# 21 additions and subtractions move from VectorE to GpSimd, and every queue gets a new order

## The chip, the cores and the metric

The kernel runs on one core of a Trainium2 chip. The core has a matrix engine (TensorE, PE in the profile, its weight loads PEld), three engines for elementwise work (VectorE = DVE, ScalarE = ACT, GpSimd = POOL) and a queue that issues DMAs (SyncE = SP). Each engine works through its own queue in order; a semaphore makes one wait for another. The metric is the device time of one execution in microseconds. Before the change it is 566.58 us, the median of three runs (565.62 to 568.13).

## The reference

Banded attention with block summaries, followed by an MLP with GELU, all in float32:

```python
q, k, v: (4, 8, 768, 64)                      # batch, heads, positions, dims
k_sum = k.reshape(B, H, 24, 32, 64).max(axis=3);  v_sum = v.reshape(B, H, 24, 32, 64).mean(axis=3)
scores_l = q @ k.T / 8, only where |i - j| < 16        # the band
scores_s = q @ k_sum.T / 8 + log(32)                   # 24 summaries for each position
a = softmax over both together
x = (a @ concat(v, v_sum)) as (3072, 512)
g = gelu(x @ w_in)                            # w_in (512, 2048)
out = g @ w_out                               # w_out (2048, 512)
```

## The kernel before

Each float32 factor of a large matmul is split into a high and a low half of 16 bits, and a product takes three matmuls (high × high, high × low, low × high). The high parts are casts, on ScalarE or GpSimd; the low parts are a difference (`*_lo`), on VectorE. So every product hangs on a chain: a read of PSUM, a cast, a difference, then TensorE.

The attention is cut into 24 units (four heads, 256 positions): `load_q`, `load_k`, `load_v` fetch, `q_hi`, `q_lo`, `k_hi`, `k_lo` split, `scores` multiplies, `maximum`, `exponent`, `recip` make the softmax, `p_hi` or `split_hi` and `p_lo` or `split_lo` split it, `turn` transposes it by DMA into `pt`, `values` multiplies with v. Two units make a chunk of 256 rows of x, two chunks a pair. For pairs 2 to 5 the first MLP product is done by Strassen's scheme: seven products (`product p j m`) instead of eight, of sums of the four blocks of x (`sx_add`) and of w_in (`t_add`); `keep` and `h_add` put the results together. Before that, `phase1` does a chunk's block with 24 matmuls and `phase1h` half of one; the first units use float32 matmuls. GELU gives g, `g_hi` and `g_lo` split it, and `phase2 c i` sums a quarter of an output block (12 matmuls of 512 columns). For the last pair the second product is done by the same scheme: sums of g (`s_add j n`, with `s_hi` and `s_lo` for the split) and of w_out (`u_add`), products `s_product m j` and `s_last`. `warm` are dummy matmuls at the start.

The four sums of a set are made in place, one out of the other: S1 into block 22, S3 into block 21, S2 from S1 into block 11, S4 from S2 into block 12. So the four `s_add j n` (n = 1, 3, 2, 4), and likewise the four `sx_add`, are a chain.

Nothing schedules this: the text `ORDER` lists 1,585 steps, and the program issues each step's instructions in that order, so that each engine's queue is the list restricted to that engine. SyncE's DMAs stand in the same list. The steps that the change touches are `q_lo` (line 723), `sx_add` (893) and `s_add` (1039); all three end in one VectorE instruction of 128 partitions × 512 columns.

Of the kernel before, what the change touches and what calls it, by code (L numbers as in the profile page):

```python
# [78 lines left out]
p_turn 0 0, wi_hi 7 1, maximum_p 1, wh_bits 6 1 1, wh_bits 6 1 2, wi_lo 1 1, wh_bits 6 0 1, exponent_p 1, wi_hi 1 0,
wh_bits 6 0 2, wi_lo 7 1, wh_bits 7 0 2, recip 1, p_norm 1, p_turn 0 1, warm 4 5, sum_vt 0, mean_vt 0, load_v 0,  # L80
load_v 1, fetch_w_in 3, fetch_w_in 5, load_q 3, sum_vt 1, wi_lo 1 0, wi_bits 2 0, load_neg, wi_hi 7 0, wi_bits 2 1,
wi_lo 7 0, f_mask 2, scores 2, p_keep 0 1, wi_hi 6 0, maximum_p 2, wi_lo 6 0, p_keep 0 0, s_load_vs 0, mean_vt 1,
warm 5 1, values 0, load_vs 1, take_hi 0, wi_hi 6 1, take_lo 0, wi_bits 3 0, wi_bits 2 2, wi_bits 3 1, wi_bits 3 2,
p_turn 1 0, p_turn 1 1, p_keep 1 0, phase1h 0 6 0, p_keep 1 1, exponent_p 2, wi_hi 2 0, wi_bits 5 0, recip 2,
values 1, phase1h 0 1 0, phase1h 0 7 0, take_hi 1, wi_hi 2 1, s_norm 2, wi_hi 3 0, wi_lo 2 0, take_lo 1, wi_bits 5 1,
f_mask 3, scores 3, fetch_w_in 4, wi_bits 5 2, t_add 3 0, maximum_p 3, wi_lo 2 1, wi_bits 4 0, wi_lo 3 0, wi_lo 6 1,
load_v 2, p_turn 2 0, phase1h 0 1 1, p_turn 2 1, wi_hi 5 1, p_keep 2 0, wi_hi 5 0, p_keep 2 1, exponent_p 3, load_q 4,
fetch_w_in 0, load_vs 2, phase1h 0 2 0, values 2, phase1h 0 7 1, phase1h 0 6 1, wi_hi 3 1, take_hi 2, gelu 0 1,
wi_bits 0 0, wi_bits 4 1, recip 3, p_norm 3, wi_bits 4 2, wi_hi 4 1, wi_bits 0 1, wi_bits 0 2, phase1h 0 3 0,
gelu 0 7, f_mask 4, scores 4, fetch_w_out 4, load_v 4, load_v 3, fetch_kx 3 0, load_q 5, fetch_w_out 0, wi_hi 4 0,  # L90
load_vs 3, s_load_vs 4, take_lo 2, maximum_p 4, wi_lo 4 0, wi_lo 3 1, p_turn 3 0, g_hi 0 7, p_keep 3 0, p_turn 3 1,
p_keep 3 1, phase1h 0 2 1, values 3, v_hi 4, gelu 0 2, wi_hi 0 0, take_hi 3, g_lo 0 7, wi_lo 4 1, phase1h 0 4 0,
take_lo 3, phase1 1 3, phase1 1 1, exponent_p 4, wo_bits 4 0, wi_hi 0 1, wi_lo 5 0, wo_bits 4 1, wi_lo 0 0,
wo_bits 4 2, wo_hi 4, wi_lo 5 1, recip 4, t_add 0 0, v_lo 4, wi_lo 0 1, f_mask 5, scores 5, wo_lo 4, gelu 1 1,
g_hi 0 2, wo_bits 0 0, g_lo 0 2, phase1h 0 4 1, wo_bits 0 1, wo_bits 0 2, g_hi 0 1, gelu 1 3, gelu 0 6, gelu 0 4,
g_hi 1 1, g_hi 1 3, g_hi 0 6, phase1 1 0, phase1 1 6, wo_hi 0, phase1h 0 0 0, phase1h 0 5 0, phase1h 0 3 1,
phase1h 0 5 1, phase1h 0 0 1, g_hi 0 4, split_hi 4, g_lo 1 1, g_lo 0 6, wo_lo 0, fetch_w_out 1, wo_bits 1 0,
wo_bits 1 1, wo_bits 1 2, g_lo 0 1, g_lo 1 3, load_v 5, load_q 7, s_load_vs 5, fetch_w_out 7, fetch_w_out 5, wo_hi 1,
# [5 lines left out]
g_lo 0 4, g_lo 0 5, wo_lo 3, fetch_w_out 6, wo_bits 6 0, wo_bits 6 1, g_lo 1 2, wo_bits 6 2, g_hi 1 5, wo_hi 6,
maximum_p 5, exponent_p 5, fetch_k 1 0, wo_lo 6, load_k 7, load_k 6, fetch_k 1 1, g_lo 1 5, split_lo 4, v_lo 5,
turn 4 1, prep_k 1 0, s_k_hi 7, recip 5, phase2 1 1, phase2 0 0, phase2 1 0, phase2 0 1, s_q_hi 6, k_hi 6, s_q_hi 7,
phase2 0 2, phase2 0 4, phase2 0 3, phase2 0 6, phase2 0 5, phase2 1 3, q_lo 7, prep_k_end 1 0, k_lo 6, q_lo 6,
k_sums 1 0, store 0 0, split_hi 5, scores 6, values 4, prep_k 1 1, add_mask 6, k_lo 7, split_lo 5, take_hi 4,
take_lo 4, prep_k_end 1 1, maximum 6, k_sums 1 1, exponent 6, phase2 1 5, phase2 1 2, phase2 0 7, scores 7,
fetch_v 1 0, load_v 6, load_k 8, fetch_v 1 1, turn 5 0, turn 5 1, load_q 8, load_k 9, load_q 9, prep_v 1 0,  # L110
prep_v 1 1, values 5, take_hi 5, load_vs 6, fetch_v 3 0, s_q_hi 8, s_k_hi 8, add_mask 7, take_lo 5, q_hi 9, s_k_hi 9,
recip 6, k_lo 8, prep_kx 3 0, k_lo 9, maximum 7, q_lo 8, split_hi 6, v_hi 6, store 0 1, phase2 1 4, phase1 2 2,
phase1 2 6, phase1 2 4, scores 8, gelu 2 2, v_lo 6, split_lo 6, g_lo 1 7, turn 6 0, put 0 0, load_v 7, turn 6 1,
load_vs 7, load_q 10, fetch_v 2 0, prep_v 3 0, add_mask 8, exponent 7, g_hi 2 2, phase1 2 3, gelu 2 3, phase2 1 7,
store 1 1, gelu 2 6, g_lo 2 2, recip 7, v_hi 7, maximum 8, p_norm 7, q_lo 9, p_hi 7, values 6, phase1 2 0, phase1 2 1,
scores 9, load_k 10, load_k 11, put 0 1, turn 7 0, v_lo 7, load_v 8, load_q 11, prep_v 2 0, p_lo 7, add_mask 9,
k_hi 10, k_hi 11, turn 7 1, q_hi 11, s_q_hi 10, k_lo 10, phase1 2 5, phase2 1 6, gelu 2 4, take_hi 6, take_lo 6,
values 7, exponent 8, g_hi 2 4, g_hi 2 6, g_lo 2 4, g_lo 2 6, gelu 2 1, g_hi 2 1, store 1 0, load_vs 8, phase1 2 7,
maximum 9, recip 8, q_lo 10, scores 10, v_hi 8, gelu 2 0, take_hi 7, gelu 2 5, split_hi 8, v_lo 8, take_lo 7,
split_lo 8, phase1 3 7, phase1 3 5, phase1 3 0, phase1 3 2, exponent 9, fetch_k 2 0, g_lo 2 1, k_lo 11, prep_k 2 0,  # L120
g_hi 2 5, g_hi 2 0, load_v 9, load_q 12, q_lo 11, t_add 2 0, t_add 0 1, g_lo 2 5, add_mask 10, g_lo 2 0, load_vs 9,
v_hi 9, gelu 3 0, gelu 2 7, g_hi 2 7, gelu 3 5, g_hi 3 0, recip 9, maximum 10, v_lo 9, put 1 0, load_k 12,
fetch_k 2 1, prep_k 2 1, g_lo 3 0, prep_k_end 2 1, turn 8 0, p_norm 9, fetch_v 2 1, turn 8 1, load_v 10, fetch_v 3 1,
exponent 10, prep_k_end 2 0, g_hi 2 3, k_sums 2 0, phase2 2 1, phase1 3 3, scores 11, values 8, gelu 3 3, g_hi 3 3,
x_take 8, phase1 3 1, load_q 13, prep_v 2 1, recip 10, p_norm 10, g_lo 2 3, phase2 2 3, phase2 2 5, sx_hi 2 0,
q_hi 12, p_hi 9, p_lo 9, q_lo 12, k_hi 12, t_add 2 1, g_lo 2 7, load_k 13, turn 9 0, s_p_hi 10, load_vs 10, turn 9 1,
gelu 3 2, gelu 3 7, add_mask 11, gelu 3 1, v_hi 10, maximum 11, s_k_hi 13, s_q_hi 13, k_lo 12, v_lo 10, p_lo 10,
phase2 2 7, sx_lo 2 0, k_sums 2 1, g_hi 3 5, store 2 1, t_add 0 2, t_add 0 3, t_add 2 2, t_add 3 1, values 9,
load_k 14, load_v 11, scores 12, phase1 3 4, g_lo 3 5, prep_v 3 1, add_mask 12, exponent 11, s_k_hi 14, k_lo 13,
q_lo 13, recip 11, load_vs 11, turn 10 0, v_hi 11, x_take 9, k_lo 14, phase2 2 0, sx_hi 2 1, split_hi 11, maximum 12,  # L130
product 2 0 1, phase2 2 2, phase1 3 6, keep 2 0 0, sx_lo 2 1, turn 10 1, load_q 14, q_hi 14, q_lo 14, split_lo 11,
load_q 15, put 1 1, product 2 0 2, values 10, turn 11 0, turn 11 1, scores 13, g_hi 3 2, g_lo 3 2, v_lo 11,
# [1141 lines left out]
```

## Time and profile before

| | |
|---|---|
| runs | 565.62, 566.58, 568.13 us, median 566.58 |
| span of the profiled execution | 564.2 us; its time with what lies around the span was not taken, the median is 2.4 us above the span |
| TensorE | 557.3 us busy, granted clock 1.000 |
| VectorE | 452.5 us busy, 699 instructions |
| ScalarE | 394.6 us busy |
| GpSimd | 39.9 us busy, 50 instructions |
| HBM | 108 GB/s over the span, 335 to 410 in the first three fortieths |

A busy share is an average over stages with different limits. TensorE's is that of matmuls whose ends are modelled, so a short wait can lie under the end of the matmul before it. The views used below are the waits (who ended the idle time of an engine), the timeline (instructions in order of time), the chain of waits (the work that ended last, followed back), the groups by line, and the busy times of a stretch. A name such as `L908` is line 908 of the kernel before.

### The profile page before, as it was taken

Reading aid. Unit: us, or ns where it says so; the run is one execution under the profiler, and the core shown is the slowest. Engines: PE = TensorE matmul, PEld = TensorE weight load, DVE = VectorE, ACT = ScalarE, POOL = GpSimd, SP = SyncE. Lnnn points to the kernel's source line nnn. Section 1 sums busy time; section 2 is a strip of 40 time slices with the busy share of each in tenths; the row PEclk is TensorE's granted clock in tenths of the full one; section 3 lists DMA queues with packets and bytes.
Section 4 is the critical chain, followed back from the end, with each engine's and each line's share of the span. In section 5 each row is a group of like instructions: output and inputs, shape, how many; then the busy total and the mean of one; then the engine's idle time right before and its main releaser. Section 6 shows DMA issues by size and latency. Waiting matters only on the chain.

```text
span 564.2 us, 14587 instructions
## 1 busy us (share of the span) xinstructions
PE 557.3 (99%) x6126; PEld 392.5 (70%) x6126; DVE 452.5 (80%) x699; ACT 394.6 (70%) x950; POOL 39.9 (7%) x50
## 2 busy tenths in 40 slices
...
GB/s 335 410 324 255 137 210 218 118 256 234 232 163 287 123 138 123 169 95 198 106 121 46 93 112 166 63 2 33 70 120 101 57 2 1 19 1 38 1 1 94
DMA packets 70993, 74.39 MB, mean 132 GB/s; under 512 B 44816, under 2 KB 49808, under 8 KB 70928
## 3 DMA queue, kind: packets, MB, share of 16 engines
...
q8 instruction: 48, 0.79, 0.6%
...
HBM read 54.90 MB, written 6.29 MB: 108 GB/s over the span
## 4 chain that ended last, share of the span: by engine, by line
PE 78%; DVE 13%; DMA 6%; ACT 1%; issue 1%; SPq 0%; ACTq 0%; DVEq 0%
PE bank L967 26%; PE bank L1022 9%; PE bank L1023 9%; PE bank L1024 9%; PE bank L1127 5%; PE ps_v L873 3%; PE ps_s L758 2%; PE bank L926 2%; PE bank L927 2%; PE bank L928 2%; DMA w_out_l<-in_kp_first_dram 2%; PE bank L939 2%; PE ps_v L1127 2%; DMA pt<-p_h 2%; DVE k L382 2%; DVE k L386 2%
## 5 line engine op out<-in xcount | busy, mean ns | idle before, releaser
L1022 PE MATMUL bank<-w_out_h,gh 128*128 128x512 f16 x320 | 121.4, 379 | 0.0
L1023 PE MATMUL bank<-w_out_l,gh 128*128 128x512 f16 x320 | 121.3, 379 | 0.0
L1024 PE MATMUL bank<-w_out_h,gl 128*128 128x512 f16 x320 | 121.3, 379 | 0.0
L1009 DVE SCALAR_TENSOR_TENSOR gl<-g,gh 128x512 f16<-128x512 f32 x92 | 63.4, 701 | 23.5 <-ACT gh L1005 23.5
L967 PEld LDWEIGHTS <-w 128*128 128x128 f16 x640 | 62.1, 98 | 10.5
L967 PEld LDWEIGHTS <-w_in 128*128 128x128 f16 x576 | 55.5, 98 | 10.3 <-issue 0.9
L1024 PEld LDWEIGHTS <-gl 128*128 128x128 f16 x320 | 31.3, 98 | 37.9 <-DVE gl L1009 0.3
L1005 ACT ACTIVATE gh<-g 128x512 f16<-128x512 f32 x92 | 55.5, 622 | 2.8 <-PE bank L1023 2.0
L786 ACT ACTIVATE s<-s,s_top 128x128 f32<-128x128 f32 x144 | 55.7, 388 | 2.3 <-DVE s_top L777 2.0
L1022 PEld LDWEIGHTS <-gh 128*128 128x128 f16 x320 | 31.3, 98 | 32.6
L1023 PEld LDWEIGHTS <-gh 128*128 128x128 f16 x320 | 31.3, 98 | 32.2
L979 DVE TENSOR_TENSOR g<-bank,late 128x512 f32<-128x512 f32 x48 | 32.9, 686 | 25.5 <-PE bank L967 19.2
L973 ACT ACTIVATE late<-bank 128x512 f32<-128x512 f32 x48 | 28.1, 590 | 31.0 <-PE bank L967 17.5
L967 PE MATMUL bank<-x,w_in 128*128 128x256 f16 x384 | 46.7, 273 | 0.7 <-DVE x L908 0.7
L967 PE MATMUL bank<-stage,w 128*128 128x256 f16 x320 | 44.1, 273 | 0.0
L967 PE MATMUL bank<-x,w 128*128 128x256 f16 x320 | 43.6, 273 | 0.0
L998 ACT ACTIVATE g<-g 128x512 f32<-128x512 f32 x48 | 29.4, 624 | 15.3 <-DVE g L979 15.3
L926 PE MATMUL bank<-x,w_in 128*128 128x256 f16 x144 | 39.3, 273 | 0.0
L927 PE MATMUL bank<-x,w_in 128*128 128x256 f16 x144 | 39.3, 273 | 0.0
L928 PE MATMUL bank<-x,w_in 128*128 128x256 f16 x144 | 39.3, 273 | 0.0
L998 ACT ACTIVATE g<-bank 128x512 f32<-128x512 f32 x48 | 27.5, 591 | 13.8 <-PE bank L967 9.7
L848 DVE SCALAR_TENSOR_TENSOR v_hl<-v,v_hl 128x1024 f16<-128x1024 f32 x20 | 24.4, 1221 | 7.6 <-ACT v_hl L845 7.6
...
## 6 DMA issues: line engine op xcount, KB each, us to landing
...
```

The lines of the kernel that those rows point to most:

```text
L786: nc.scalar.activation(self.s32[:, gs], score[:, gs], AF.Exp, bias=self.top[:, g : g + 1], scale=QKSCALE, accum_out=self.den[:, g : g + 1],)
L926: nc.tensor.matmul(dst, wh, xh, start=(k == 0), stop=False)
L927: nc.tensor.matmul(dst, wh, xl, start=False, stop=False)
L928: nc.tensor.matmul(dst, wl, xh, start=False, stop=(k == NCC - 1))
L967: nc.tensor.matmul(dst, l, r[:, k], start=(first and e == 0 and k == 0 and n == 0), stop=(k == KH - 1 and n == 2), skip_group_check=True,)
L998: nc.scalar.activation(g, h, AF.Gelu, scale=1.0 / (SC_X * SC_WI))
L1005: nc.scalar.activation(gh, g_slot(c, i), AF.Copy, scale=SC_G)
L1009: nc.vector.scalar_tensor_tensor(out=gl, in0=g_slot(c, i), scalar=SC_G, in1=gh, op0=ALU.mult, op1=ALU.subtract)
L1022: nc.tensor.matmul(t, gh[:, f, js], w_out_h[:, f, :], start=(n == 0), stop=False)
L1023: nc.tensor.matmul(t, gh[:, f, js], w_out_l[:, f, :], start=False, stop=False)
L1024: nc.tensor.matmul(t, gl[:, f, js], w_out_h[:, f, :], start=False, stop=(n == NFC - 1))
L1127: nc.tensor.matmul(acc[:, t * NH : (t + 1) * NH], a[:, f, js], b[:, f], start=(first and j == 0 and t == 0 and f == 0 and n == 0), stop=(f ...
```

## The change

`q_lo`, `sx_add` and `s_add` get a parameter for the engine, and three new steps call them with GpSimd:

```diff
+        def g_q_lo(self):
+            self.q_lo(nc.gpsimd)
+
+        def q_lo(self, engine=nc.vector):
+            engine.tensor_tensor(out=self.ql, in0=self.q32, in1=self.qh, op=ALU.subtract)
...
+    def g_sx_add(p, n):
+        sx_add(p, n, nc.gpsimd)
+
+    def sx_add(p, n, engine=nc.vector):
...
-        nc.vector.tensor_tensor(out=out, in0=in0, in1=in1, op=op)
+        engine.tensor_tensor(out=out, in0=in0, in1=in1, op=op)
...
+    def g_s_add(j, n):
+        s_add(j, n, nc.gpsimd)
+
+    def s_add(j, n, engine=nc.vector):
...
-        nc.vector.tensor_tensor(out=seen[out], in0=seen[in0], in1=seen[in1], op=op)
+        engine.tensor_tensor(out=seen[out], in0=seen[in0], in1=seen[in1], op=op)
```

The list `ORDER` is a new one throughout. It has the same 1,585 steps, but 21 of them by their new names: `g_q_lo` for units 14, 16, 18, 20 and 22, `g_sx_add 3` and `g_sx_add 4` (n = 3, 4, 5, 6), `g_s_add 2` and `g_s_add 3` (n = 1 to 4). Two lines of it, the start of the old and of the new:

```diff
-fetch_k 0 0, load_m16, prep_k 0 0, load_q 0, warm 0 12, f_mask 0, warm 1 1, scores 0, maximum_p 0, exponent_p 0,
+load_q 0, fetch_k 0 0, load_m16, fetch_wh 7 1, prep_k 0 0, warm 4 5, warm 0 12, warm 5 1, f_mask 0, scores 0,
```

Three places in the order, as the built programs have it (before, then now; lines of the kernel after are 3 to 12 higher).

SyncE, the first loads of the kernel before: `q` are the queries of units 0 and 1, `w_out_l` from `in_kp_first` the keys of the first batch in two halves (`fetch_k 0 0`, `fetch_k 0 1`), the rows from `in_w_in` raw halves or blocks of w_in.

```order
L518 DMA w_out_l<-in_kp_first_dram 128x2x864
L349 DMA mask_sb<-in_mask_dram 128x664
L643 DMA q_0_83<-in_qd_dram 128x512
L431 DMA stage<-in_w_in_dram 128x2x512
L352 DMA w_out_h<-in_mask_dram 128x272
L431 DMA gl_107<-in_w_in_dram 128x2x512 x2
L431 DMA stage<-in_w_in_dram 128x2x512 x2
L518 DMA w_out_l<-in_kp_first_dram 128x2x864
L643 DMA q_1_84<-in_qd_dram 128x512
```

SyncE, the first loads now:

```order
L646 DMA q_0_83<-in_qd_dram 128x512
L521 DMA w_out_l<-in_kp_first_dram 128x2x864
L352 DMA mask_sb<-in_mask_dram 128x664
L434 DMA stage<-in_w_in_dram 128x2x512
L646 DMA q_1_84<-in_qd_dram 128x512
L419 DMA gh_108<-in_w_in_dram 128x4x512
L521 DMA w_out_l<-in_kp_first_dram 128x2x864
L358 DMA mask_sb<-in_mask_dram 128x128
L355 DMA w_out_h<-in_mask_dram 128x272
L434 DMA gl_107<-in_w_in_dram 128x2x512
```

The second half of the keys moved from behind five half blocks of w_in to behind one half block and one whole block; the first half stands behind a load of queries.

VectorE near the end, before, from `g_lo 11 7` on: `g_…` are the buffers of g, `gl_109` and `gl_107` low halves of g of chunks 11 and 10, `w_3` low halves of the sums of j = 3, `v_hl` and `k` sums of w_out and `pt` a low half of one.

```order
L1009 SCALAR_TENSOR_TENSOR gl_109<-g_0_101,gh_108 128x512
L1044 TENSOR_TENSOR g_0_101<-g_2_103,g_0_101 128x512
L1044 TENSOR_TENSOR g_2_103<-g_1_102,g_2_103 128x512
L1044 TENSOR_TENSOR g_1_102<-g_0_101,g_1_102 128x512
L1089 TENSOR_TENSOR v_hl_115<-v_hl_115,w_out_l 128x512
L979 TENSOR_TENSOR g_3_104<-bank_64,late 128x512
L1061 SCALAR_TENSOR_TENSOR w_3_78<-g_1_102,w_2_77 128x512
L1096 TENSOR_TENSOR pt<-k_82,pt 128x512
L1061 SCALAR_TENSOR_TENSOR w_3_78<-g_2_103,w_2_77 128x512
L1009 SCALAR_TENSOR_TENSOR gl_107<-g_3_104,gh_106 128x512
```

VectorE near the end now, from `s_lo 2 2` to `s_lo 3 1`:

```order
L1073 SCALAR_TENSOR_TENSOR w_2_77<-g_1_102,w_1_76 128x512
L1073 SCALAR_TENSOR_TENSOR w_2_77<-g_2_103,w_1_76 128x512
L988 TENSOR_TENSOR g_2_103<-bank_63,late 128x512
L1101 TENSOR_TENSOR v_hl_115<-v_hl_115,w_out_l 128x512
L1018 SCALAR_TENSOR_TENSOR gl_109<-g_4_105,gh_108 128x512
L1018 SCALAR_TENSOR_TENSOR gl_107<-g_2_103,gh_106 128x512
L1108 TENSOR_TENSOR p_l<-v_hl_115,p_l 128x512
L1073 SCALAR_TENSOR_TENSOR w_3_78<-g_1_102,w_2_77 128x512
L1073 SCALAR_TENSOR_TENSOR w_3_78<-g_0_101,w_2_77 128x512
L1073 SCALAR_TENSOR_TENSOR gl_109<-g_4_105,gh_108 128x512
```

The three L1044 rows (`s_add 3 1`, `3 3`, `3 2`) are gone from behind `g_lo 11 7`, which is the fifth row here; the low halves of the sums of j = 3 stand last.

GpSimd's last instructions now, `g_s_add 2 1`, `2 3`, `2 2`, `2 4` and then `3 1`, `3 3`, `3 2`, `3 4` (before, its last ones were casts of x):

```order
L1056 TENSOR_TENSOR g_4_105<-g_2_103,g_4_105 128x512
L1056 TENSOR_TENSOR g_2_103<-g_1_102,g_2_103 128x512
L1056 TENSOR_TENSOR g_1_102<-g_4_105,g_1_102 128x512
L1056 TENSOR_TENSOR g_3_104<-g_3_104,g_1_102 128x512
L1056 TENSOR_TENSOR g_4_105<-g_1_102,g_4_105 128x512
L1056 TENSOR_TENSOR g_1_102<-g_0_101,g_1_102 128x512
L1056 TENSOR_TENSOR g_0_101<-g_4_105,g_0_101 128x512
L1056 TENSOR_TENSOR g_2_103<-g_2_103,g_0_101 128x512
```

The two chains of four stand directly behind one another, nothing between them.

## Rows read from the trace of the kernel before

**Rows 1.** The page, busy us (share of the span) and instructions of each engine.

```profile
PE 557.3 (99%) x6126; PEld 392.5 (70%) x6126; DVE 452.5 (80%) x699; ACT 394.6 (70%) x950; POOL 39.9 (7%) x50
```

**Rows 2.** The waits of TensorE: us in total, times, longest us.

```profile
PE bank L915 <- POOL ones L358: 0.9, 1, 0.9
PE ps_s L740 <- DVE ks L528: 0.7, 1, 0.7
PE bank L967 <- DVE x L908: 0.7, 1, 0.7
PE ps_v L873 <- DMA pt<-p_l: 0.6, 1, 0.6
PE ps_s L740 <- issue: 0.5, 1, 0.5
PE ps_v L873 <- DMA pt<-p_h: 0.2, 1, 0.2
```

**Rows 3.** The timeline of VectorE, first 19 us: start, us, instruction [idle before].

```profile
5.24 1.75 DVE L528 TENSOR_REDUCE ks<-w_out_l 128x48 f32<-128x1536 f32 x1 [5.24 <-DMA w_out_l<-in_kp_first_dram]
...
16.56 1.75 DVE L528 TENSOR_REDUCE ks<-w_out_l 128x48 f32<-128x1536 f32 x1 [0.76 <-DMA w_out_l<-in_kp_first_dram]
```

**Rows 4.** Groups by line and form, VectorE, weights and maxima: busy us, mean ns.

```profile
L774 DVE TENSOR_REDUCE s_top<-ps_s 128x8 f32<-128x1024 f32 x6 | 7.3, 1219 | 2.0 <-PE ps_s L740 1.9
...
L377 DVE TENSOR_SCALAR w<-stage 128x512 int32<-128x512 int32 x4 | 1.6, 422 | 0.5 <-DMA stage<-in_w_in_dram 0.5
...
L386 DVE SCALAR_TENSOR_TENSOR w<-gh,w 128x1024 int32<-128x1024 int32 x2 | 2.4, 1222 | 0.0
...
L377 DVE TENSOR_SCALAR w<-gh 128x1024 int32<-128x1024 int32 x2 | 1.4, 688 | 0.0
```

**Rows 5.** The chain of waits, 124 to 132 us: start, us, what.

```profile
122.33 5.96 DMA pt<-p_l
```

**Rows 6.** The timeline near 205 us.

```profile
204.18 0.69 DVE L908 TENSOR_TENSOR x<-stage,x 128x512 f16<-128x512 f32 x1
...
204.92 0.49 PE L967 MATMUL bank<-x,w_in 128*128 128x256 f16 x3 [0.69 <-DVE x L908]
```

**Rows 7.** Groups by line and form, all engines.

```profile
L1005 ACT ACTIVATE gh<-g 128x512 f16<-128x512 f32 x92 | 55.5, 622 | 2.8 <-PE bank L1023 2.0
...
L967 PE MATMUL bank<-x,w_in 128*128 128x256 f16 x384 | 46.7, 273 | 0.7 <-DVE x L908 0.7
...
L1044 DVE TENSOR_TENSOR g<-g,g 128x512 f32<-128x512 f32 x16 | 11.0, 689 | 0.7 <-ACT g L998 0.3
...
L672 POOL COPY v_hl<-w_out_l 24x1024 f32<-24x1024 f32 x2 | 3.3, 1644 | 42.9 <-ACT w_out_l L576 29.0 <-DMA v_hl<-in_vw_dram 13.9
...
L905 POOL CAST x<-den 128x512 f16<-128x512 f32 x1 | 0.6, 609 | 0.0
```

**Rows 8.** Busy us of each engine by stretch: PE, PEld, DVE, ACT, POOL.

```profile
30.00:130.00 100.00, 98.76 (x1273) 71.56 (x1266) 97.89 (x134) 72.41 (x185) 5.12 (x4) 1.00 0.69 216
285.00:312.00 27.00, 27.00 (x329) 19.94 (x327) 21.69 (x36) 19.96 (x46) 3.50 (x4) 1.00 0.33 89
365.00:405.00 40.00, 40.00 (x386) 25.57 (x385) 24.55 (x44) 24.79 (x59) 3.78 (x4) 1.00 0.15 34
500.00:545.00 45.00, 45.00 (x380) 36.89 (x378) 33.16 (x52) 23.77 (x44) 0.00 (x0) 1.00 0.03 13
```

**Rows 9.** The timeline of GpSimd beside VectorE, near 131 and 299 us.

```profile
131.18 0.79 DVE L719 TENSOR_TENSOR k_lo<-k,k_hi 128x640 f16<-128x640 f32 x1
131.29 1.15 POOL L713 CAST qh<-q 128x512 f16<-128x512 f32 x1 [17.23 <-DVE s_rec L798]
...
299.49 0.61 POOL L905 CAST stage<-den 128x512 f16<-128x512 f32 x1
299.57 1.07 DVE L908 TENSOR_TENSOR stage<-stage 128x512 f16<-128x512 f32 x1 [0.71 <-POOL stage L905]
```

**Rows 10.** The chain of waits in the last 32 us.

```profile
546.66 1.31 PE ps_v L1127 x12
```

More of the change, by code (lines that the diff above doesn't have):

```diff
@@ L79 @@
[L79 to L98, printed above, removed]
@@ L104 @@
[L104 to L123, printed above, removed]
@@ L124 @@
[L124 to L132, printed above, removed]
-h_add 2 0 0, add_mask 13, exponent 12, recip 12, g_lo 3 3, t_add 2 3, g_hi 3 1, x_take 10, gelu 4 0, p_norm 12,
@@ new lines @@
+sx_lo 2 4, recip 13, sx_lo 2 5, sx_add 2 6, s_q_hi 15, add_mask 14, maximum 14, t_lo 0 0, t_lo 0 1, q_lo 15,
+phase2 3 3, phase2 3 7, store 3 1, phase2 3 2, product 2 1 2, sx_hi 2 6, split_hi 13, turn 12 1, k_lo 15, v_lo 12,
+t_hi 1 0, product 2 0 6, keep 2 0 1, product 2 2 1, scores 15, exponent 14, t_lo 1 0, split_lo 13, h_add 2 1 0,
+sx_hi 2 3, s_k_hi 16, recip 14, sx_lo 2 3, add_mask 15, t_add 3 2, put 3 1, values 12, load_k 17, turn 13 0,
+turn 13 1, product 2 0 7, phase2 3 4, phase2 3 6, maximum 15, keep 2 2 0, g_hi 4 0, g_lo 4 0, keep 2 0 2, t_hi 1 1,
```

270 lines of the change are left out of this document (157 added, 113 removed).

## The prediction

> **What bounds the kernel now.** Four views, in this order. The page's busy times first: TensorE is busy 557.3 us of a span of 564.2, VectorE 452.5, ScalarE 394.6, GpSimd 39.9 [rows 1]. TensorE's row alone leaves 6.9 us idle. Then the waits of TensorE: 0.9 us before its first instruction, and inside the span five waits: 0.7 for `ks`, 0.7 for `x`, 0.6 and 0.2 for `pt`, 0.5 for nothing that the profile shows [rows 2]. That is 2.7 us. The remaining 3.3 (6.9 − 0.9 − 2.7) lie behind the last matmul. Then the places of the three waits that have a releaser: near 17, 128 and 205 us [rows 3, 5, 6]. Last the busy times by stretch: from 30 to 130 us VectorE is busy 97.89 of 100, from 285 us on much less: 21.69 of 27, 24.55 of 40, 33.16 of 45 [rows 8].
>
> So the span is TensorE's queue plus its few waits. The change alters neither the matmuls nor their number. What it can give is at most those 2.7 us (a little more, since the modelled end of a matmul hides the start of a wait), and what it can cost is every new wait. The profile has no outside time of its own; the median of the three runs, 566.58, is 2.4 us above the profiled span, and I carry these 2.4 unchanged.
>
> **The 21 moved operations.** Off VectorE go 21 instructions of 512 columns at 0.69 us [rows 7] (the L1044 row; the five low parts of q take as long): 14.5 us. Of that I count nothing as gain: the sums of x and g stand behind 285 us, where VectorE idles a fifth to two fifths of the time and TensorE shows no wait at all [rows 2, 8], and the low parts of q are a few per cent of VectorE's work around them. On GpSimd come 21 additions with two inputs, which the trace does not show. From below: a cast of 512 columns, one input, takes 0.61 when it is alone [rows 7] (the L905 row). From above: a GpSimd copy of 1,024 columns takes 1.64 [rows 7] (the L672 row). I take 1.22, two reads of 0.61, near the middle. 21 × 1.22 = 25.6 us, so GpSimd is busy 65 of 564 us: no bound by itself. What is queued behind an addition on GpSimd is the next addition or cast of the same chain, and ScalarE's casts wait for it.
>
> There is a second price. At 299.49 us a GpSimd cast runs while VectorE's L908, which reads two arrays in SBUF, starts at 299.57: it takes 1.07 instead of 0.69. At 131.29 the other way round: a GpSimd cast starts while VectorE's L719 runs and takes 1.15 instead of 0.61 [rows 9]. One waits until the other is done. So an addition that leaves VectorE can still hold it for up to 1.22 us.
> The Trainium skill (GPSIMD Engine Reference, § 4.1 Engine selection) speaks against the change: elementwise work with two inputs belongs on VectorE, GpSimd being about twice as slow. Its side-by-side figure in § 3.1 (4497 ns against 2293 for 2,048 columns) gives, as an estimate, 1.12 us for 512; by it the chain of three below would be 0.3 us shorter. No row here shows such an addition.
>
> **Where the chains of additions are covered.** Pair 3: TensorE's order has behind `values 15` and before `product 3 0 6` three products (1.31 each), three quarter blocks of the output (12 matmuls of 512 columns, 2.6 each) and two short steps (0.8 and 0.9), 13.4 us. The chain that must be done by then is a read of PSUM, a cast, a low part, three additions, a cast and a low part: 0.6 + 0.6 + 0.7 + 3 × 1.22 + 0.6 + 0.7 = 6.9, and 2 to 3 more if the lock strikes at each addition. Covered; if that cover went it would cost 1.22 per addition. For pair 4 the cover is eight quarter blocks, over 20 us.
> The end is tighter. Count from T, the end of `product 5 3 3` on TensorE. Nine products at 1.31 [rows 10] stand before `s_product 6 3`, so it starts at T + 11.8, and it needs the low part S2 of j = 3. ScalarE reaches `g_hi 11 7` at about T + 2.5 (its instructions there take 0.62 each, the L1005 row of [rows 7], behind a store that waits for the quarter block before `product 5 3 3`). VectorE, in its new order, then has five rows to and with `g_lo 11 7`, done at about T + 4.7. Then the three additions, with one VectorE row before each of the first two because of the lock: 2 × 0.69 + 3 × 1.22 = 5.0, T + 9.7. ScalarE's cast 0.62, T + 10.3, and VectorE's low part 0.69, T + 11.0, or, if the fourth addition holds it, T + 12.3. Against T + 11.8 that is between 0.8 early and 0.5 late. I take +0.3. It lies on the path: nothing behind it can catch up.
>
> **What the new order does to the waits.**
> `ks` at 17 us. VectorE's second reduction waited 0.76 us for its load [rows 3], then TensorE for it. SyncE had 4,846 KB issued up to and with that load, the first load being 864 KB, done at 5.24; so (4846 − 864) / (16.56 − 5.24) = 352 KB/us. Now 3,942 KB stand there, 256 of them before the first load. The first lands at 5.24 + 256/352 = 6.0, the second at 6.0 + (3942 − 1120)/352 = 14.0. VectorE's queue between its two reductions is now 0.42 + 2 × 0.69, a maximum of 1.22, a low part of 0.69, and 0.69 + 2 × 1.22 [rows 4], in all 6.8; behind the first reduction (6.0 + 1.75), with a little for the scores that the maximum reads, it ends near 14.9, the second reduction at 16.7. TensorE arrives at about 17, as five dummy matmuls went ahead of it and five behind. The wait falls from 0.7 to about 0.1: −0.6. VectorE has 0.3 us to spare, no more.
> `x` at 205 us. `sx_lo 2 1` ended at 204.87 and TensorE had stopped 0.69 us for it [rows 6]. By sums over the queues VectorE now reaches it 3 us later, but TensorE reaches `product 2 0 2` 13 us later (behind `values 11` now, not before `values 10`): −0.7.
> `pt` at 128 us. The last transposition was issued at 122.33 and landed 5.96 us later [rows 5]. VectorE's sum of row durations before `split_lo 5` falls by 7.0 us, TensorE's before `values 5` by 4.4; the distance grows by 2.6, more than the 0.8 waited. SyncE has only one load between the two transpositions, so nothing queues before it: −0.8.
> The 0.5 without a releaser I leave.
> New waits. Everything got new neighbours, 328 steps of TensorE among them, and I can't follow each. From below 0, from above as much as the old order had, 2.7; I take 1.0, a third, since the three places that I followed came out with time to spare.
>
> Sum: −0.6 − 0.7 − 0.8 + 0.3 + 1.0 = −0.8. Span 564.2 − 0.8 = 563.4, with 2.4 outside it 565.8. About 0.5%, 2.8 us, is what a measurement of this kernel can tell from no change; the forecast is no change, 0.8 us to the good.
>
> **The rivals.**
> Faster: all of the waits inside the span go and none comes: 566.6 − 2.7 = 563.9, and up to 0.8 us more because each wait is hidden for 0.16 us behind the modelled end of a matmul (0.27 long, the L967 row of [rows 7], 1.31/12 = 0.11 apart [rows 10]): 563.1. For it: the three places above are all relieved by the queues' sums. Against it: the 0.5 has no releaser that an order could move, and the old order of the same steps had five. Chance 0.24.
> Slower by GpSimd at the end: if an addition takes what the slowest row suggests, 1.64, the chain of three ends 3 × 0.42 = 1.3 later, and if the lock then holds VectorE for 1.64 at four rows more there (1.64 − 0.69 each, 3.8), the end moves by 0.3 + 1.3 + 3.8, 5.4 instead of 0.3; with the rest of the sum 565.8 + 5.1 = 570.9. It decides from 1.4 us per addition on, where the 0.8 to spare is gone. For it: the 1.07 and 1.15 of [rows 9]. Against it: VectorE idles 27% of that stretch [rows 8]. Chance 0.12.
> Slower by VectorE's queue at the start: the loads of the other weights come later than before (`fetch_wh 1 1` as the tenth load, 4,654 KB, at 16.0 us by the same rate; before as the sixth, 2,446 KB). If such a load is 4 us late, VectorE, in order, stands still, and as it is busy 97.89 of 100 us up to 130 [rows 8] it can't make it up; TensorE then waits as long: 565.8 + 4 = 569.8. It decides where a load comes over 1 us after VectorE reaches it. For it: only 0.3 us to spare at 17 us. Against it: DMA moved 352 KB/us just there, and 16.0 is before VectorE's 16.7, when it can first ask for them. Chance 0.11.
> That the change does not do what it says is no case: the order shows all 21 on GpSimd.
>
> **How the numbers follow.** Forecast 0.53, faster 0.24, the two slower 0.12 and 0.11. Within the forecast the unknown waits (0 to 2.7) and the end (−0 to +0.5 around 0.3) give 564.5 to 567.7, the likeliest case's own range. The range that holds 8 in 10 reaches to the faster case's end and to the slower ones: 563.0 to 570.5. Faster by over 0.5% needs under 563.75: nearly all of the faster case, 0.22. Slower by over 0.5%, above 569.4: most of the two slower cases, 0.20. The rest, 0.58, within.
>
> **What would show it.** Right: TensorE's waits in the profile after no longer name `ks`, `x` at `product 2 0 2`, or `pt` at `values 5`; VectorE's busy time is 14 us lower, less what the lock adds to its L1018 and L1073 rows; GpSimd's additions have a median near 1.2 us; TensorE's busy share stays at 99%. Wrong: a wait of TensorE for `w` or `gl` from S2 of j = 3 in the last 25 us (the end), for weights in the first 60 us (the start), or a row of VectorE that waits for a load there. If GpSimd's additions take under 0.8 or over 1.6 us, the price was wrong. If the span changes by more than 3 us without new waits, then TensorE's own queue is not fixed, and the whole argument falls.

## The result, and the profile of the changed kernel

The changed kernel takes 574.77 us (573.81 to 576.60) against 566.72 (565.62 to 568.13) beside it: ratio 1.0136, 95% interval 1.0101 to 1.0172. It is slower, by 8 us, outside the predicted range (563.0 to 570.5); the forecast was no change. Every ratio here and below is to the kernel before, run beside the kernel in question (medians 566.72 to 567.50 us). One execution below was slow (582.45 us); it is left out of its ratio, but stands in the median of 571.15. The profiled execution spans 572.0 us, 7.8 more than before.

The page of the changed kernel, busy us of each engine (answers to [rows 1]):

```profile
PE 557.1 (97%) x6126; PEld 392.5 (69%) x6126; DVE 454.7 (79%) x678; ACT 393.1 (69%) x950; POOL 68.4 (12%) x71
```

TensorE has the same 6126 matmuls and the same busy time, but 97% in place of 99. VectorE did not become 14 us shorter: with 21 instructions fewer it is busy 2.2 us longer. GpSimd took on 28.5 us.

The waits of TensorE in the changed kernel, us in total, times, longest us (answers to [rows 2]):

```profile
PE ps_v L879 <- DMA pt<-p_h: 4.9, 4, 1.7
PE ps_v L879 <- DMA pt<-p_l: 2.0, 2, 1.1
PE bank L976 <- ACT ot L1037: 1.8, 1, 1.8
PE bank L924 <- POOL ones L361: 0.9, 1, 0.9
PE ps_s L764 <- DVE k_lo L722: 0.7, 1, 0.7
PE bank L1139 <- DVE w L1073: 0.7, 1, 0.7
PE bank L1031 <- ACT gh L1014: 0.5, 1, 0.5
PE bank L976 <- DVE g L988: 0.2, 1, 0.2
```

Without the row for `ones`, which was there before, this is 10.8 us; before it was 2.7. All of the old ones are gone (`ks`, the `x` of `product 2 0 2`, the `pt` of `values 5`, and the 0.5 without a releaser), and 10.8 − 2.7 = 8.1 is the whole difference of the spans, 7.8. So it is a matter of new waits alone, and 6.9 of them are for `pt`: the transposed attention weights. By place, from the gaps between matmul starts (less the regular spacing): 1.3 us at 143 (unit 6), 1.9 at 171 (unit 8), 2.9 at 196 (unit 9), 1.4 at 303 (unit 16), 0.4 at 367 (unit 19); for `k_lo` 0.9 at 160; for `ot` 2.0 at 396; for `w` 0.8 at 549. 7.0 us of that lie before 203.6 us, where GpSimd's first addition starts.

SyncE's queue ahead of unit 9's transpositions (start, us, instruction; SPq is SyncE issuing):

```profile
177.97 1.00 SPq L591 DMA_DIRECT2D stage<-in_vb_dram  x2
181.97 0.35 SPq L661 DMA_DIRECT2D v<-in_vw_dram  x1
186.63 0.31 SPq L591 DMA_DIRECT2D stage<-in_vb_dram  x1
...
188.27 1.66 SPq L848 DMA_TRANSPOSE pt<-p_h  x1
...
191.68 3.15 SPq L848 DMA_TRANSPOSE pt<-p_l  x1
```

and the chain of waits there:

```profile
177.97 6.32 DMA stage<-in_vb_dram
...
184.32 2.28 DVE vm L599
...
191.68 5.80 DMA pt<-p_l
```

The halves of unit 9 were ready at 174.47 and 179.81 us. But `load_v 10` waits on SyncE until 181.97 and `fetch_v 2 1` until 186.63, since its staging buffer is read by VectorE's L599 until then, and the two transpositions stand behind them: issued at 188.27 and 191.68, landed at 197.48. TensorE was there at 194.50.

Busy us by stretch (PE, PEld, DVE, ACT, POOL; answers to [rows 8]):

```profile
365.00:405.00 40.00, 37.23 (x390) 22.04 (x389) 32.21 (x54) 25.98 (x70) 10.14 (x10) 1.00 0.28 72
```

From 365 to 405 us VectorE is busy 32.21 where it was 24.55, although additions left it (it runs 54 instructions there, not 44, as the order is another). The timeline shows what it does (VectorE, then GpSimd, then ScalarE):

```profile
377.64 1.75 DVE L917 TENSOR_TENSOR x<-stage,x 128x512 f16<-128x512 f32 x1 [2.27 <-POOL x L914]
379.31 1.75 DVE L1018 SCALAR_TENSOR_TENSOR gl<-g,gh 128x512 f16<-128x512 f32 x1
380.99 4.24 DVE L814 SCALAR_TENSOR_TENSOR p_l<-s,s_rec,p_h 128x128 f16<-128x128 f32 x8
...
386.47 0.68 DVE L988 TENSOR_TENSOR g<-bank,late 128x512 f32<-128x512 f32 x1
...
377.57 1.26 POOL L908 TENSOR_TENSOR stage<-den,stage 128x512 f32<-128x512 f32 x1
378.91 1.60 POOL L908 TENSOR_TENSOR den<-stage,den 128x512 f32<-128x512 f32 x1
...
387.19 0.63 ACT L1007 ACTIVATE g<-g 128x512 f32<-128x512 f32 x1 [6.22 <-DVE g L988]
```

L917 and L1018, 0.69 us elsewhere, take 1.75 beside an addition on GpSimd (L908), and the eight parts of `split_lo 20` take 4.24 in place of 2.2: together 4.2 of the 7.7 us that this stretch gained. Of these 4.2 some 3.1 are from additions; the first three parts of `split_lo 20` ran beside GpSimd's casts (L914, 0.69 each, 0.34 without), only the fourth beside an addition (1.35). Behind all of these stands `h_add 3 3 1` (L988), and ScalarE has waited 6.22 us for it; ScalarE's `exponent 22` and then `store 6 1` follow, for which TensorE stops at 396.

GpSimd's additions by line and form (busy us, mean ns of one):

```profile
L1056 POOL TENSOR_TENSOR g<-g,g 128x512 f32<-128x512 f32 x8 | 11.8, 1472 | 74.1 <-ACT g L1007 62.7 <-DVE gl L1018 11.0
...
L730 POOL TENSOR_TENSOR ql<-q,qh 128x512 f16<-128x512 f32 x5 | 6.4, 1285 | 0.2
```

All 21 take 31.1 us, 1.48 each.

And the chain of waits at the end:

```profile
542.38 1.28 POOL g L1056
...
543.73 1.60 POOL g L1056
...
547.04 0.64 ACT w L1069
...
547.70 1.54 DVE w L1073
...
549.29 1.26 PE bank L1139 x10
```

The additions `g_s_add 3 1` and `3 3`, ScalarE's cast, and VectorE's low part at 1.54 in place of 0.69 lead to TensorE's wait for `w`, 0.7 us.

### The profile page after: what moved, and what is told of

It reads as the page before. It is cut to its first block, busy times and chain, and to the rows that moved or that the text cites. A ratio compares the mean times of both kernels' runs of the same rounds, so it can differ in the third digit from the quotient of the medians.

```text
span 572.0 us, 14587 instructions
## 1 busy us (share of the span) xinstructions
PE 557.1 (97%) x6126; PEld 392.5 (69%) x6126; DVE 454.7 (79%) x678; ACT 393.1 (69%) x950; POOL 68.4 (12%) x71
## 4 chain that ended last, share of the span: by engine, by line
PE 64%; DVE 15%; DMA 10%; ACT 4%; issue 2%; SPq 2%; POOL 2%; POOLq 0%; DVEq 0%; ACTq 0%
PE bank L976 21%; PE bank L1031 7%; PE bank L1033 7%; PE bank L1032 7%; PE bank L948 4%; DMA v<-in_vw_dram 3%; PE bank L1139 3%; DMA stage<-in_vb_dram 3%; PE ps_v L879 3%; PE bank L924 2%; DVE gl L1018 2%; PE ps_s L746 2%; PE ps_v L1139 2%; DVE p_l L814 2%; DVE v_hl L854 1%
## 5 line engine op out<-in xcount | busy, mean ns | idle before, releaser
L1018 DVE SCALAR_TENSOR_TENSOR gl<-g,gh 128x512 f16<-128x512 f32 x92 | 65.1, 722 | 24.5 <-ACT gh L1014 24.4
L988 DVE TENSOR_TENSOR g<-bank,late 128x512 f32<-128x512 f32 x48 | 32.8, 685 | 23.7 <-PE bank L976 14.3
```

The lines of the kernel that those rows point to most:

```text
L988: nc.vector.tensor_tensor(out=g, in0=acc(p, j, a), in1=hsum[s], op=ALU.add)
L1018: nc.vector.scalar_tensor_tensor(out=gl, in0=g_slot(c, i), scalar=SC_G, in1=gh, op0=ALU.mult, op1=ALU.subtract)
```

## Experiments

Theory O: the new order puts single steps late in queues that run in order, transpositions above all. Theory G: the additions on GpSimd, and what they hold up on VectorE, cost the time.

**Engine and order apart.** Additions back on VectorE, the new order kept:

```diff
-            self.q_lo(nc.gpsimd)
+            self.q_lo()
...
-        sx_add(p, n, nc.gpsimd)
+        sx_add(p, n)
...
-        s_add(j, n, nc.gpsimd)
+        s_add(j, n)
```

> The changed kernel's order, with the 21 additions back on VectorE at the same places. Theory O (the order: transpositions stand in SyncE's queue behind loads that wait, and values 6 stands too close behind its transposition): the stalls of TensorE at 143, 160, 171 and 196 us, where GpSimd has done no addition yet, stay to the tenth (7.0 us in sum); so do those at 303 and 367 us (1.8), 573 to 574.5 us in all. Theory G (the engine: additions of about 1.5 us and the lock against VectorE): VectorE's busy time falls by some 10 us and the time to 566 to 568 us. A mixture, which I hold for likeliest: the stalls before 205 us stay, those from 288 us on (6.2 us, the 2.0 for ot at 396 us above all) go for the most part: about 570 us.

Measured 587.14 us, ratio to before 1.0329 (1.0289 to 1.0368): 12 us slower than the changed kernel, which no theory expected. TensorE's longest wait, and VectorE's timeline near it:

```profile
PE ps_s L764 <- DVE ql L730: 6.8, 1, 6.8
```

```profile
379.37 1.23 DVE L854 SCALAR_TENSOR_TENSOR v_hl<-v,v_hl 128x1024 f16<-128x1024 f32 x1 [5.45 <-ACT v_hl L851]
...
383.75 1.09 DVE L730 TENSOR_TENSOR ql<-q,qh 128x512 f16<-128x512 f32 x1
```

The waits up to 205 us stayed in sum, as O said (2.1, 0.6, 2.2 and 2.4 us by matmul starts, 7.3 against 7.0), though not one by one. New is 6.8 us for `ql`: the low part of q of unit 22 ran on GpSimd at 332.18 us in the changed kernel; on VectorE it stands behind `v_lo 20` and is done at 384.84. TensorE's clock is halved (granted 0.50) from 380.5 us, inside this wait, to 390.7, and behind two waits for `pt` from 144.9 to 148.3 and from 199.5 to 203.0. Its busy time is 562.8 us, 5.7 more than in the changed kernel; 6.8 + 5.7 is most of the 13.5 by which the spans of the two profiled executions differ. By the length of the stretches in which it worked at 0.50 (5.8, 3.4 and 3.4 us) about half of the 5.7 belongs to `ql`; that is an estimate. The order is written for GpSimd's nearly empty queue.

The page of this kernel shows what the additions do to VectorE:

```profile
PE 562.8 (96%) x6126; PEld 395.3 (68%) x6126; DVE 453.9 (78%) x699; ACT 393.8 (67%) x950; POOL 39.0 (7%) x50
```

In the same order VectorE is busy 453.9 us with the 21 additions and 454.7 without them: what it no longer does itself, 14.5 us, it spends in instructions that take longer beside GpSimd, about 0.7 us for each addition there.

The other way round, the old order with the same 21 on GpSimd (functions of the changed kernel):

```diff
-product 2 0 1, phase2 2 2, phase1 3 6, keep 2 0 0, sx_lo 2 1, turn 10 1, load_q 14, q_hi 14, q_lo 14, split_lo 11,
+product 2 0 1, phase2 2 2, phase1 3 6, keep 2 0 0, sx_lo 2 1, turn 10 1, load_q 14, q_hi 14, g_q_lo 14, split_lo 11,
...
```

> The order of the kernel before, with the same 21 additions on GpSimd at the places where VectorE had them. Theory O: 566.5 to 567.5 us, as before, and TensorE's waits are those of before (2.7 us inside the span). Theory G: 571 to 574 us, new waits of TensorE from 285 us on and at the end. The mixture: 568 to 570 us, nothing new before 205 us, 2 to 3 us of new waits behind it.

Measured 570.28 us, ratio 1.0062 (1.0040 to 1.0084); the mixture, a little above its upper end. TensorE's longest wait, and VectorE and GpSimd near it:

```profile
PE bank L973 <- DVE x L914: 2.1, 1, 2.1
```

```profile
205.31 0.83 DVE L780 TENSOR_SCALAR s_top<-s_top 128x8 f32<-128x8 f32 x1
206.06 0.68 DVE L914 TENSOR_TENSOR x<-stage,x 128x512 f16<-128x512 f32 x1
...
204.97 1.15 POOL L727 TENSOR_TENSOR ql<-q,qh 128x512 f16<-128x512 f32 x1
```

A scaling of 8 columns takes 0.83 us, until the addition on GpSimd is over, where it took 0.17 in the kernel before, and `sx_lo 2 1` starts that much later: a part of the 1.4 by which the wait for `x` grew; the rest I can't place. Others are new at the end, 0.5 + 0.4, both for a sum of w_out (`pt`). VectorE is busy 446.1 us here, 6.3 less than before: in this order the lock took back less than in the new one. So the engine alone costs about 3 us in the old order, the new order 8 with GpSimd's additions, and 20 without them. The two do not add up.

**Transpositions ahead.** In the changed kernel `turn 8 0`, `turn 9 0`, `turn 9 1`, `turn 16 0` and `turn 19 0` go ahead of the loads, `values 6` one step back:

```diff
-phase2 2 1, scores 11, v_lo 9, fetch_v 2 0, prep_v 2 0, g_lo 2 7, fetch_v 3 1, load_v 10, fetch_v 2 1, load_k 13,
-s_q_hi 13, q_lo 13, load_q 15, turn 9 0, load_vs 10, turn 9 1, fetch_kx 3 2, add_mask 11, exponent 10, gelu 3 0,
+phase2 2 1, scores 11, v_lo 9, turn 9 0, fetch_v 2 0, prep_v 2 0, g_lo 2 7, fetch_v 3 1, turn 9 1, load_v 10, fetch_v 2 1, load_k 13,
+s_q_hi 13, q_lo 13, load_q 15, load_vs 10, fetch_kx 3 2, add_mask 11, exponent 10, gelu 3 0,
...
```

> The changed kernel, additions on GpSimd; five transpositions (units 8, 9 twice, 16, 19) moved in SyncE's queue ahead of the loads and the store that they stood behind, and values 6 one step of TensorE later. Theory O: the waits for pt at 143, 171, 196, 303 and 367 us fall from 7.9 us in sum to under 1.5, the time to about 568 us. Theory G: the wait is late data, not a late issue, so the transpositions come no earlier than their halves are done: 574 to 575 us. The loads behind them start some us later; where TensorE then waits for v instead, less is won (570 us).

Measured 572.30 us, ratio 1.0092 (1.0064 to 1.0120). The waits for `pt` fell from 6.9 to 1.4 us, as O expected; the time by 2.5 only (the two intervals overlap a little), as all waits but `ones` fell from 10.8 to 8.7. What came up, and the granted clock (PEclk, behind the busy times) behind the two longest waits, with the same for the changed kernel behind its 1.8:

```profile
PE bank L1031 <- ACT gh L1014: 2.5, 1, 2.5
PE ps_s L764 <- DVE k_lo L722: 2.2, 1, 2.2
PE ps_v L879 <- DMA pt<-p_h: 1.4, 2, 0.8
```

```profile
154.00:157.20 3.20, 3.20 (x23) 2.17 (x16) 3.20 (x3) 3.12 (x5) 1.28 (x2) 0.50 0.61 195
389.50:392.80 3.30, 3.30 (x9) 1.04 (x8) 3.27 (x6) 2.79 (x8) 0.00 (x0) 0.50 0.00 0
```

```profile
396.00:400.00 4.00, 3.97 (x100) 3.46 (x103) 3.97 (x12) 2.41 (x9) 0.00 (x0) 1.00 0.00 0
```

TensorE arrives earlier and now waits 2.2 us for VectorE's `k_lo` at 153 and 2.5 for ScalarE's `gh` at 389. Behind the two its clock is granted at 0.50, from 153.9 to 157.3 and from 389.4 to 392.8 (the lower of its two levels, 1.2 and 2.4 GHz); behind the wait of 1.8 us in the changed kernel it stays at 1.00. TensorE's busy time is 2.6 us higher than there, in an execution that is 2.2 us above its median. This differs from execution to execution: the mean clock over the runs is 0.994 to 1.000 for this kernel, and for the changed kernel too (573.81 and 574.06 us at 1.000, 575.48 at 0.997, 576.60 at 0.994). So the halved clock explains this one profile and not the small gain; that is the other waits.

Both edits together, additions on VectorE and transpositions ahead:

> Both edits together: transpositions ahead of the loads, and the 21 additions on VectorE. The mixture: what the two give adds up, 563.5 to 566 us, at or under the kernel before. Theory O alone: as the kernel with the transpositions ahead, about 568. Theory G alone: as the kernel with the additions on VectorE, 566 to 568.

Measured 581.31 us, ratio 1.0242 (1.0208 to 1.0277), far above all three expectations: the transpositions ahead give 5.8 us here, but the wait for `ql` stayed (6.3). Whether this is one place or VectorE's load was tried with `g_q_lo 22` alone left on GpSimd, twenty additions on VectorE:

```diff
-            self.q_lo(nc.gpsimd)
+            self.q_lo(nc.gpsimd if self.nm == "22" else nc.vector)
...
```

> The changed kernel's order with twenty additions on VectorE and only the low part of q of unit 22 on GpSimd. Theory Q: the 7.1 us wait for ql at 385 us in the kernel with all 21 on VectorE came from one place in VectorE's queue (the low part stood behind v_lo 20, which waits for its v); it goes, with the halved clock behind it: 575 to 578 us, near the changed kernel's 574.8. If VectorE's load is what costs, the wait comes back elsewhere: 582 us or more.

Measured 578.72 us, ratio 1.0188 (1.0156 to 1.0219), just above what Q expected: the 6.8 us are gone and the time is 8.4 lower, but 3.2 for `late` and 1.5 for `g` are there near 262, 272 and 334 us, where the changed kernel has none or 0.2. The first of them, from the chain of waits near 255 us:

```profile
253.02 0.61 DVE ql L730
...
253.65 0.33 SPq L646
...
254.96 3.06 DMA v<-vm
...
258.12 1.06 ACT v_hl L851
```

The low part of q of unit 16 runs at 252.94 on VectorE (on GpSimd it ran at 228.75 in the changed kernel). `load_q 18` waits for it on SyncE (issued at 253.65, not 244.94), the load of v behind it comes late, and ScalarE waits 2.7 us for this v and copies `late` behind it, while VectorE itself stands idle for 2.65. So most of the loss was one place, and at least this part of the rest is another of the same kind; that VectorE's load costs anything here is not shown.

**What stood behind the transpositions.** Four more steps moved, on GpSimd's version:

```diff
-v_lo 7, take_hi 6, g_hi 2 1, gelu 2 3, s_k_hi 9, g_hi 2 3, prep_k 2 0, g_lo 2 1, k_lo 9, take_lo 6, turn 7 1,
+v_lo 7, take_hi 6, g_hi 2 1, gelu 2 3, s_k_hi 9, g_hi 2 3, g_lo 2 1, k_lo 9, prep_k 2 0, take_lo 6, turn 7 1,
...
-g_sx_add 4 3, q_hi 23, p_sx_hi 4 1, sx_lo 4 1, g_lo 6 3, product 3 3 3, split_lo 20, g_sx_add 4 5, g_sx_add 4 4,
+g_sx_add 4 3, q_hi 23, p_sx_hi 4 1, sx_lo 4 1, g_lo 6 3, product 3 3 3, h_add 3 3 1, split_lo 20, g_sx_add 4 5, g_sx_add 4 4,
...
```

> The kernel with the transpositions ahead, additions on GpSimd, with four more steps moved: turn 15 0 and turn 11 0 ahead of their second halves, prep_k 2 0 behind k_lo 9 in VectorE's queue, h_add 3 3 1 ahead of split_lo 20 there. Theory Q (what is left of the loss are single steps behind an in-order queue: SyncE's loads and VectorE's own): the waits for k_lo at 153 us (2.4), for gh at 389 us (2.6) and for pt at 217 and 288 us (1.8) go, and the stretches of halved clock behind the first two with them: 563.5 to 566 us, no slower than the kernel before. Theory G (additions and lock set the time in the stretch from 375 to 400 us whatever the order): the wait at 389 us stays within 1 us, about 569 us. If waits only move on to other places, 568 to 571 us.

Measured 572.64 us, ratio 1.0090 (1.0067 to 1.0113): nothing won, a miss.

```profile
PE ps_s L764 <- DVE k_lo L722: 1.9, 1, 1.9
PE bank L976 <- ACT ot L1037: 1.8, 1, 1.8
```

No wait for `pt` is left, but `k_lo 10` took the place of `k_lo 9` (with the clock at 0.50 behind it, from 161.0 to 164.5), `gl` that of `gh` (1.4), and the 1.8 for `ot` is back. Then the eight additions of g were put on VectorE in that kernel:

> The same, with the eight additions of g back on VectorE at the places the order gives them; the thirteen others stay on GpSimd. The 0.8 us that TensorE waits at 550 us for w (three GpSimd additions of 1.3 to 1.6 us and their locks) go: 0.6 to 0.9 us less than the kernel before it in this list. If GpSimd's additions are not the cause there, nothing changes.

571.43 us, ratio 1.0073 (1.0048 to 1.0097). The wait for `w` is gone; the times differ by 1.2 us with overlapping intervals. The 1.8 for `ot` stands in this kernel too and, what decides it, in the one with twenty additions on VectorE, where no addition on GpSimd is near. So I had put it down wrongly to GpSimd: `store 6 1` stands behind `exponent 22` in ScalarE's order though its data are there 5 us before (in the changed kernel its last matmul ends at 390.30, it runs at 395.40).

Twelve more steps, in the queues of VectorE and ScalarE, two of the places (against the changed kernel, so that the earlier move of `turn 16 0` shows too):

```diff
-u_add 0 3, sx_hi 4 6, sx_lo 4 3, sx_lo 4 6, u_hi 0 0, u_lo 0 0, exponent 22, recip 22, q_lo 23, phase2 6 4,
-phase2 6 2, phase2 6 1, phase2 7 1, phase2 6 3, phase2 6 5, phase2 6 7, phase2 6 6, g_hi 7 2, keep 4 0 0, sx_lo 4 5,
+u_add 0 3, sx_hi 4 6, sx_lo 4 3, sx_lo 4 6, u_hi 0 0, u_lo 0 0, q_lo 23, phase2 6 4,
+phase2 6 2, phase2 6 1, phase2 7 1, phase2 6 3, phase2 6 5, phase2 6 7, phase2 6 6, store 6 1, exponent 22, recip 22, g_hi 7 2, keep 4 0 0, sx_lo 4 5,
...
-g_lo 5 5, h_add 3 0 0, add_mask 18, sx_lo 3 4, sx_lo 3 5, product 3 1 1, phase2 4 7, load_v 17, turn 16 0,
+g_lo 5 5, h_add 3 0 0, sx_lo 3 4, add_mask 18, sx_lo 3 5, product 3 1 1, phase2 4 7, load_v 17,
...
```

> The kernel with the transpositions ahead, the additions of g on VectorE and thirteen additions on GpSimd (571.4), with twelve more steps moved in the queues of VectorE and ScalarE, each ahead of what it stood behind where TensorE waited for it: store 6 1 ahead of exponent 22 (the wait of 2.0 us at 394), k_lo 10 and add_mask 9 (1.7 at 161), add_mask 13 and v_lo 11 (1.2 and 0.8 at 216 to 220), sx_lo 3 4 (0.9 at 303), g_lo 6 7 (0.7 at 387), h_add 2 3 3 (0.5 at 288). Theory Q (single steps late in in-order queues, no engine at its limit): those 7.8 us go but for what comes up behind them, 564 to 567 us, level with the kernel before. Theory V (VectorE has too much to do from 125 to 225 us, so waits only move): the waits at 394, 303, 387 and 288 go (4.1 us), those up to 225 us come back at other steps: 567.5 to 569 us.

Measured 567.78 us, ratio 1.0010 (0.9998 to 1.0022): level with the kernel before, with thirteen additions on GpSimd. Waits of TensorE:

```profile
PE bank L976 <- ACT late L982: 1.6, 2, 1.3
PE bank L976 <- DVE w L480: 1.2, 1, 1.2
...
PE bank L976 <- DVE x L917: 0.8, 1, 0.8
PE ps_v L879 <- DVE v_hl L854: 0.6, 2, 0.5
PE bank L935 <- ACT g L1007: 0.4, 1, 0.4
```

4.6 us beside the 0.9 for `ones`, none over 1.3, against 10.8. So the loss was these places: 22 moves in the queues of SyncE, VectorE, ScalarE and TensorE, and at the end the additions of g. The 22 moves with all 21 additions on GpSimd were not run. With the eight sums of x on VectorE as well, only the low parts of q on GpSimd:

> The kernel with twelve more steps moved (567.8), with the eight sums of x on VectorE at the same places, so that only the five low parts of q run on GpSimd. Theory G (beside a busy VectorE an addition on GpSimd costs VectorE more than the 0.69 us that it saves, as the locks at 291 to 297 and 371 to 383 us show): the waits of 1.0 us at 387 and 1.5 at 395 us for steps behind those additions shrink, 565.5 to 566.7 us. Theory R (in this order the additions are at places that suit GpSimd's queue alone, as with all 21 on VectorE): new waits of TensorE in these two stretches, 569 us or more. Nothing within 0.6 us of 567.8 would say that lock and relief cancel.

569.84 us, ratio 1.0034 (1.0014 to 1.0055). The wait for `x` at 387 us went, but `late` grew from 1.6 to 2.6, and 2.8 for `g` came up near 324 to 334 us: R, by a ratio 0.0024 higher, though the intervals just overlap. The profiled execution (571.69 us) is the slowest of its kernel, and 0.9 us of its extra waits lie at 143 us, far ahead of the edit.

**One cause put into the kernel before.** Both transpositions of unit 9 go behind `load_k 14`. They stand behind the steps that write unit 10's weights then, so that unit 9's output is made from those: that part of the computation is changed, the amount of work is not.

```diff
-q_hi 12, p_hi 9, p_lo 9, q_lo 12, k_hi 12, t_add 2 1, g_lo 2 7, load_k 13, turn 9 0, s_p_hi 10, load_vs 10, turn 9 1,
+q_hi 12, p_hi 9, p_lo 9, q_lo 12, k_hi 12, t_add 2 1, g_lo 2 7, load_k 13, s_p_hi 10, load_vs 10,
...
-phase2 2 7, sx_lo 2 0, k_sums 2 1, g_hi 3 5, store 2 1, t_add 0 2, t_add 0 3, t_add 2 2, t_add 3 1, values 9,
-load_k 14, load_v 11, scores 12, phase1 3 4, g_lo 3 5, prep_v 3 1, add_mask 12, exponent 11, s_k_hi 14, k_lo 13,
+phase2 2 7, sx_lo 2 0, k_sums 2 1, g_hi 3 5, store 2 1, t_add 0 2, t_add 0 3, t_add 2 2, t_add 3 1, load_k 14, turn 9 0, turn 9 1, values 9,
+load_v 11, scores 12, phase1 3 4, g_lo 3 5, prep_v 3 1, add_mask 12, exponent 11, s_k_hi 14, k_lo 13,
```

> The kernel before, with one thing of the new order put into it: both transpositions of unit 9 stand behind load_k 14 in SyncE's queue, which waits until 189 us for its buffer; before, they were issued at 180.2 and 183.8, values 9 began at 190.6. Theory Q: they are issued at 189.4 and 190.7, and values 9 waits some 5 us for pt: 571.5 to 574 us, the upper end if TensorE's clock is halved for some us behind the wait. If a late issue is made good by a faster transposition or by the work behind it: 567 to 569 us.

Measured 571.15 us, ratio 1.0079 (1.0059 to 1.0099). SyncE:

```profile
189.88 0.33 SPq L646 DMA_DIRECT2D k<-in_kd_dram  x1
190.33 1.27 SPq L842 DMA_TRANSPOSE pt<-p_h  x1
192.15 1.23 SPq L842 DMA_TRANSPOSE pt<-p_l  x1
```

The first was issued right behind the load, as expected, the second when `p_lo 10` was done. They landed at 193.98 and 195.01, 3.65 and 2.86 us behind their issue; TensorE stopped 2.65 + 1.0 us by matmul starts. With that the clock is granted at 0.50 from 194.5 to 197.9, and TensorE is busy 558.7 us, 1.4 more than before. The mechanism is O's; the price is about 4 us in all. The stop alone was shorter than the 5 expected, as I had taken the landing at the 5.96 of [rows 5].

**The kernel before without its waits.** Two tries, additions on VectorE; `fetch_k 0 1` and `load_q 1` one load earlier and `sx_lo 2 1` ahead of `maximum 12` in both:

```diff
-prep_v 1 1, values 5, take_hi 5, load_vs 6, fetch_v 3 0, s_q_hi 8, s_k_hi 8, add_mask 7, take_lo 5, q_hi 9, s_k_hi 9,
+prep_v 1 1, phase2 1 4, values 5, take_hi 5, load_vs 6, fetch_v 3 0, s_q_hi 8, s_k_hi 8, add_mask 7, take_lo 5, q_hi 9, s_k_hi 9,
...
```

> The kernel before, all additions on VectorE, with four edits at its own waits: fetch_k 0 1 and load_q 1 one load earlier, sx_lo 2 1 ahead of maximum 12, phase2 1 4 ahead of values 5. The waits for ks (0.9 by TensorE's spacing), q (0.25), x (0.85) and pt at 128 us (1.2) go: 564.0 us, 0.4% under the kernel before. If each wait is only replaced by one a step later: 566 to 567 us.

566.01 us, ratio 0.9990 (0.9969 to 1.0010). The second, with `k_lo 7` behind `split_lo 5` and `maximum_p 2` behind `take_lo 0` in place of the lines above:

> The kernel before with its waits taken up in another way: fetch_k 0 1 and load_q 1 one load earlier, sx_lo 2 1 ahead of maximum 12, k_lo 7 behind split_lo 5, maximum_p 2 behind take_lo 0. Against the first try (566.0, where 1.0 us came up at 34 us for take_lo 0 and 0.6 at 133 us for take_lo 5) both should be smaller: 564.5 to 565.5 us. If the waits move on once more: 566.

567.02 us, ratio 1.0004 (0.9990 to 1.0018). Both times the old waits went, and others came up (0.9 for `x` at 34 us in the first, 2.0 for `pt` in the second). No version here beats the kernel before by what can be measured.

## Why the prediction was wrong

**The step that failed: "New waits. … From below 0, from above as much as the old order had, 2.7; I take 1.0".** They are 10.1 us, and 0.7 at the end beside them. The old order's waits are no bound for another order; three places that came out well were taken for all, and of the transpositions only unit 5's were followed in SyncE's queue ("nothing queues before it" holds there). Units 9 and 16 have loads before theirs that wait for buffers; in units 8 and 19 the first half stands behind the second, which waits for its low part (SyncE waits for it from 157.7 to 163.8 and from 345.0 to 359.8 us); and `values 6` comes 4.5 us behind its last one: 6.9 of the 10.1. The frame held: the span is TensorE's queue plus its waits.

**The removals** `ks`, `x` and `pt` of `values 5` went as predicted, 2.2 us where I had 2.1. The 0.5 without a releaser went as well, which I had left.

**GpSimd's additions**, "I take 1.22": alone one takes 1.26 (the low parts of q 1.16), beside VectorE up to 2.14, in the mean 1.48. The price of the operation was near, that of the lock too small: it took back all of the 14.5 us on VectorE (453.9 us busy with the additions, 454.7 without, in the same order), where the prediction had VectorE 14 us lower, less some lock. "Of that I count nothing as gain" (of the 14.5 us) was half right: VectorE's busy time did not fall, but with the same order and all 21 on it the time is 12 us longer; an operation taken off a queue is worth what stands behind it there.

**The end**, "+0.3": +0.7. The three additions took 1.27, 1.59 and 1.60, and the low part of S2 1.53 beside the fourth.

**The rivals.** Slower by GpSimd at the end: the mechanism is there with 0.7 us, not 5.4. (Its threshold, 1.4 us per addition, does not follow from 0.8 us over three additions, which gives 1.5; the three took 1.49 in the mean. And VectorE idles 26% of that stretch by [rows 8], not 27.) Slower by VectorE's queue at the start: TensorE had no wait for weights in the first 60 us, and VectorE 0.7 us for raw blocks of w_in, where it had 0.5. The slower case that happened, transpositions behind waiting loads, was not among them. "TensorE's busy share stays at 99%" and "VectorE's busy time is 14 us lower" were the signs that failed.

Of the lock the Trainium skill (SBUF — State Buffer, § SBUF: two separate sides) says that the pair of ports is held for a whole instruction and the other engine fully blocks. The trace agrees: 1.75 us for L1018 in place of 0.69 beside an addition of 1.60.

What stays open: how the 8 us divide between the 22 moves, as they were tried in groups and a wait that goes uncovers the next; and what the thirteen additions left on GpSimd, with their lock, still cost or give.
